# An attention layer and two expert layers on one core: float64 weights loaded from ScalarE's queue, a second cast of the keys, values one item later, sums in pinned steps

## The chip, the cores and the metric

One core of a Trainium2 chip runs the whole program in one launch. The metric is device time in microseconds (us), the median of several runs; lower is better. Engines are named as in the profile: PE (TensorE matmuls), PEld (its weight loads), DVE (VectorE), ACT (ScalarE), POOL (GpSimd), SP (SyncE, which here only issues DMAs).

## The reference

Three layers follow each other. The first is causal attention with a decay: per head a bias built from a running sum of max(s, 0), clipped at zero, is added to the scaled scores.

```python
scores = scale * np.matmul(q, k.transpose(0, 1, 3, 2))      # q, k, v: (2, 8, 576, 64)
cum = np.cumsum(np.maximum(s, 0.0), axis=-1)
bias = -(cum[:, :, :, None] - cum[:, :, None, :])
scores = np.where(causal, -1000000000.0, scores + np.minimum(bias, 0.0))
attn = softmax(scores); x = np.matmul(attn, v)              # then to (1152, 512)
h = x @ w_in; x = np.maximum(0.01 * h, h) @ w_out           # w_in 512x2048, float64 on input
p = domain_probs / (domain_probs.sum(-1, keepdims=True) + 1e-09)
out = sum(p[:, e:e+1] * (np.maximum(x @ w1[e], 0.0) @ w2[e]) for e in range(4))
```

The weights w_in and w_out arrive as float64 and are read as pairs of 32-bit words; the rest is float32.

## The kernel before

**Precision.** Products run in a reduced-precision float32 format. An operand that needs full precision is kept as two terms, hi (a cast by ACT) and lo (the operand less hi, by POOL or DVE), and a product is three matmuls. In the attention's second half the scores put the terms into one tile: `ks` holds the keys' hi in partitions 0 to 63 and their lo in 64 to 127, `kd` holds the hi again in 0 to 63 and the two decay rows behind it, `qs` the queries.

**Attention.** A unit is a batch and a pair of heads (`of_unit`). Units 0 to 7 do the first 256 queries, units 8 to 15 the other 320. A unit's work is cut into items, one tile of queries by one head: four in each of the first eight units, six in the others. `attention()` walks over the items; in turn i it runs the scores of item i, the exponentials of item i - 1, the transposes of item i - 3, the values of item i - 4 and the finish of item i - 6 (`STEPS`), and yields three times, where the caller puts other work. When a unit starts, the loads of keys and values two units on are issued on SP; two turns later `split_keys` makes the next unit's terms at once: three casts or differences, then a DMA on SP that copies the keys' hi from `ks` to `kd`, then the decay rows.

**Weights of the first expert layer.** Sixteen pieces of 128x1024 float64 (`stream`) are loaded to `r64` (two buffers) in two DMAs each by `fetch64`, on SP. `converted` rebuilds float32 from the two words in five steps (ACT, then three times DVE, then the split into hi and lo and a store to the DRAM scratch `w_f32`, on SP). `supply` runs through them; the main block at the end of the function steps it between the items. For the second token group the float32 pieces are read back from `w_f32` and combined to seven sums (`seven`), on POOL.

**The order.** While `fixed` is set every instruction keeps the order in which the code issues it on its engine; the order is thus written by hand for the attention and the first token group's pass through the first expert layer. After that `fixed` is cleared, and a scheduler orders all but what `keep_in_program_order` names. `idling(2)` issues two matmuls on zeros into the unused tile `nothing`; before the change it does so in the turns up to 7.

**Paired tokens.** The second expert layer, and the second token group in the first, use products of half-size blocks of which seven do the work of eight. `paired_steps(s, ...)` makes the seven token operands `t7` from an activation: four sums on DVE and three casts with differences, twice. It runs for the attention's output (s = 1, in the main block, in steps), for the first token group's result (`paired_tokens(0, y_t[0], t7early)`, called at step 12 of `mlps(phases[1])`) and for the second's (`paired_tokens(1, y_t[1], t7pool)`). `paired_up` forms the products; its evictions on DVE are named `tmp` and `ps_u`.

Of the kernel before, what the change touches and what calls it, by code (L numbers as in the profile page):

```python
# [19 lines left out]
def attention_moe_moe2(ctx: ExitStack, tc: tile.TileContext, q, k, v, s, w_in, w_out, probs, w1, w2, out):  # L20
# [89 lines left out]
    def fetch64(n):  # L110

        src, (rows, _) = stream[n][:2]
        r64 = r64p.tile([P, 1024, 2], U32, tag="r64", name="r64")
        r64s.append(r64)
        for i in range(2):
            a, c = slice(i * rows // 2, (i + 1) * rows // 2), slice(i * 512, (i + 1) * 512)
            nc.sync.dma_start(r64[:, c].rearrange("p (a b) t -> p a (b t)", a=rows // 2), src[:, a])
            yield

    def converted(n):  # L120
# [17 lines left out]
        nc.sync.dma_start(w_f32[unit], raw)  # L138
        yield

    def supply():

        for n in range(2 * DFF // P // 2):
            yield from converted(n)
            if len(r64s) < 2 * DFF // P // 2:
                for _ in fetch64(len(r64s)):
                    pass
# [151 lines left out]
    def paired_steps(s, of, pool):  # L299
# [3 lines left out]
        for k in range(2):  # L303
# [6 lines left out]
            nc.vector.tensor_tensor(sums[:, 3], b22, b12, ALU.subtract)  # L310
            nc.vector.tensor_tensor(sums[:, 0], b21, sums[:, 2], ALU.subtract)
# [236 lines left out]
    def split_keys(n):  # L548

        qr, kr = k_raw.pop(n)  # L550
        qs = q_s[n % 2]
        nc.scalar.copy(qs[:, 0], qr)
        nc.gpsimd.tensor_tensor(qs[:D, 1], qr[:D], f32(qs[:D, 0]), ALU.subtract)
        ks = ap.tile([P, 2, S], F32R, tag="ks", name="ks")
        nc.scalar.copy(ks[:D], kr)
        nc.gpsimd.tensor_tensor(ks[D:], kr, f32(ks[:D]), ALU.subtract)
        kd = ap.tile([P, 2, S], F32R, tag="kd", name="kd")
        nc.sync.dma_start(f32(kd[:D]), f32(ks[:D]))
        k_split[n] = ks, kd, qs
        decay(n, kd)  # L560
# [11 lines left out]
    class Unit:  # L572
# [36 lines left out]
        def transposes(self, i, j):  # L609
            z = self.z.pop((i, j))  # L610
            pv = self.pv[i, j] = ap.tile([P, QT, P], F32, tag="pv", name="pv", bufs=3)[:, : i + 1]
# [45 lines left out]
    STEPS = ((Unit.scores, 0), (Unit.exps, 1), (Unit.transposes, 3), (Unit.values, 4), (Unit.finish, 6))  # L657

    def attention():

        items, starts, n = [], {}, 0
        i = 0
        while n < units or i < len(items) + 6:
            if n < units and i == len(items):
# [3 lines left out]
                if n + 2 < units and n + 2 != 2 * NP:  # L668
                    load_keys(n + 2)
                    load_values(n + 2)  # L670
# [4 lines left out]
                if n + 2 == 2 * NP:  # L675
                    load_values(n + 2)
                n += 1
            if 2 * NP <= n < units and i == starts[n - 1] + 2:
                split_keys(n)
            for step, lag in STEPS:  # L680
# [3 lines left out]
                if lag in (1, 3, 6):  # L684
# [11 lines left out]
    with ExitStack() as phase:  # L696
# [5 lines left out]
        with tc.tile_pool(name="early", bufs=1) as early:  # L702
            ones = pads(early)
            cumulative()
            loads = (x for n in range(2) for x in fetch64(n))
            main = mlps(phases[0])

            for at_ in range(3 * 64):
# [5 lines left out]
                if at_ % 3 == 1:  # L714
                    if i < 8:
# [92 lines left out]
```

## Time and profile before

| | |
|---|---|
| median of 3 runs | 759.5 us (759.05 to 760.18) |
| the profiled execution | 758.02 us, its span 756.2 us |
| mean granted TensorE clock | 0.981 of full speed |
| busy PE / PEld | 718.1 us (95%) / 649.6 us (86%) |
| busy DVE / ACT / POOL | 415.5 (55%) / 321.0 (42%) / 322.8 us (43%) |
| moved by DMA | 66.50 MB, mean 88 GB/s |
| chain that ended last | PE 80%, DVE 6%, ACT 6%, issue 3%, DMA 3%, POOL 1% |

The page's strip of 40 slices (18.9 us each) shows PE under 9 tenths in slices 2, 4, 14, 15, 17 and the last, and at 9 in all others; the granted clock is under 9 tenths in slices 2, 4 and 14. Shares over the whole span therefore say little: the attention fills the first 227 us, the hand-over to the second token group runs to some 312 us, and the rest is matmul behind matmul. Windows and timelines of these stages are what is read. All lines of the kernel's engine calls carry the number of the recording helper (L43), so tiles tell the places apart.

### The profile page before, as it was taken

To read this page: it belongs to the slowest core of one execution; us is meant where nothing else is said; L and a number is where in the kernel's file an instruction comes from. 1 tells how busy PE (TensorE), PEld (TensorE's weight loads), DVE (VectorE), ACT (ScalarE), POOL (GpSimd) and SP (SyncE) were. 2 spreads that over 40 slices of the span, in tenths; PEclk is the share of its full clock that TensorE was granted. 3 is DMA by queue.
4 is the path that set the end of the run, shared out by engine and by line. 5 is a ranking of instruction groups with operands and counts; after the bars stand their busy time and mean duration, and the time that the engine had idled before them with its cause. 6 is when DMAs were issued, how large, how long until landed. Compare 5 with 4: busy or idle time off the path is not lost.

```text
span 756.2 us, 11325 instructions
## 1 busy us (share of the span) xinstructions
PE 718.1 (95%) x4340; PEld 649.6 (86%) x4340; DVE 415.5 (55%) x850; ACT 321.0 (42%) x635; POOL 322.8 (43%) x250
## 2 busy tenths in 40 slices
PE   9694999999999889899999999999999999999997
PEld 8573789888887679899998998988989889898996
DVE  4654765757658766644574454544535445354452
ACT  4563877676564465543343231412314123142210
POOL 4122544434218758867427261462614526144200
PEclk9897999999999899999999999999999999999999
DMA  5795567664333222221212120111101111020002
GB/s 146 203 216 136 164 150 191 190 177 156 123 128 129 68 85 84 84 84 57 57 48 65 45 67 1 56 56 54 59 1 57 56 55 56 1 60 25 1 29 97
DMA packets 40346, 66.50 MB, mean 88 GB/s; under 512 B 4228, under 2 KB 23204, under 8 KB 40292
## 3 DMA queue, kind: packets, MB, share of 16 engines
q1 hardware_dynamic: 40292, 65.78, 30.0%
q8 instruction: 34, 0.56, 0.3%
q14 instruction: 20, 0.16, 0.1%
HBM read 52.58 MB, written 10.82 MB: 84 GB/s over the span
## 4 chain that ended last, share of the span: by engine, by line
PE 80%; DVE 6%; ACT 6%; issue 3%; DMA 3%; POOL 1%; SPq 0%; ACTq 0%; POOLq 0%; DVEq 0%
PE ps_d L43 35%; PE ps_u L43 32%; PE ps_o L43 5%; PE ps_sc L43 3%; PE ps_pt L43 3%; DVE raw L43 2%; PE nothing L43 1%; DMA kd<-ks 1%; DVE sums L43 1%; DVE t L43 1%; ACT w L43 1%; DMA r<-in_moe_w_in_dram 1%; ACT ht L43 1%; ACT raw L43 1%; ACT t L43 1%
## 5 line engine op out<-in xcount | busy, mean ns | idle before, releaser
L43 POOL TENSOR_TENSOR w<-raw,w 128x1024 fp32r<-128x1024 f32 (+2 forms) x88 | 147.5, 1690 | 350.8 <-ACT w L43 328.5
L43 PE MATMUL ps_u<-t,w 128*128 128x320 f32 (+1 forms) x1680 | 239.1, 300 | 5.5 <-DVE tmp L43 2.6
L43 PEld LDWEIGHTS ps_u<-t,w 128*128 128x128 f32 x1680 | 234.7, 190 | 9.9 <-DVE tmp L43 3.1
L43 PE MATMUL ps_d<-w,ht 128*128 128x512 f32 x864 | 203.3, 391 | 0.0
L43 PEld LDWEIGHTS ps_d<-w,ht 128*128 128x128 f32 x864 | 160.2, 188 | 31.9
L43 ACT ACTIVATE ht<-ps_u 128x320 fp32r<-128x320 f32 (+2 forms) x176 | 74.2, 433 | 164.3 <-DVE ps_u L43 133.5
L43 PE MATMUL ps_d<-ht,w 128*128 128x320 f32 (+1 forms) x576 | 114.1, 347 | 4.3 <-DVE ht L43 2.1
L43 ACT CAST w<-raw 128x1024 fp32r<-128x1024 f32 (+2 forms) x88 | 64.0, 757 | 97.8 <-PE ps_d L43 77.0
L43 DVE SCALAR_TENSOR_TENSOR oacc<-ps_d,pn,oacc 128x512 f32<-128x512 f32 x63 | 47.3, 751 | 104.3 <-PE ps_d L43 104.3
L43 PEld LDWEIGHTS ps_d<-ht,w 128*128 128x128 f32 x576 | 93.0, 192 | 12.5 <-DVE ht L43 2.9
L43 PEld LDWEIGHTS ps_o<-vs,pv 128*128 128x128 f32 x480 | 64.9, 195 | 12.4 <-ACT pv L43 3.7
L43 DVE TENSOR_TENSOR ps_u<-ps_u,tmp 128x320 f32<-128x320 f32 (+1 forms) x120 | 56.1, 471 | 26.7 <-PE ps_u L43 25.2
L43 PE MATMUL ps_o<-vs,pv 128*128 128x65 f32 x480 | 64.4, 271 | 4.9 <-ACT pv L43 2.2
L43 DVE SCALAR_TENSOR_TENSOR ht<-ps_u,ht 128x320 fp32r<-128x320 f32 (+1 forms) x128 | 56.4, 453 | 22.8 <-ACT ht L43 21.3
L43 DVE CUSTOM_DVE_ANT_0 z<-ps_sc,mask 128x256 f32<-128x256 f32 (+4 forms) x80 | 40.7, 513 | 39.9 <-PE ps_sc L43 31.5
L43 POOL TENSOR_TENSOR w<-sums,w 128x1024 fp32r<-128x1024 f32 x24 | 57.8, 2408 | 6.8 <-ACT w L43 6.8
L43 DVE TENSOR_TENSOR tmp<-ps_u,tmp 128x320 f32<-128x320 f32 (+1 forms) x80 | 36.7, 464 | 41.0 <-PE ps_u L43 39.1
L43 ACT ACTIVATE z<-z,mn 128x256 f32<-128x256 f32 (+4 forms) x80 | 48.5, 607 | 22.8 <-DVE mn L43 22.7
L43 PE MATMUL ps_u<-x,w 128*128 128x512 f32 x192 | 57.8, 416 | 0.1
L43 ACT COPY pv<-ps_pt 128x512 f32<-128x512 f32 (+3 forms) x96 | 38.8, 422 | 24.1 <-PE ps_pt L43 23.8
L43 PE MATMUL ps_pt<-ident,z 128*128 128x128 f32 x240 | 41.2, 279 | 6.5 <-ACT pv L43 6.3
L43 DVE TENSOR_TENSOR ht<-ps_u,ht 128x320 fp32r<-128x320 f32 (+1 forms) x48 | 26.5, 555 | 35.6 <-ACT ps_u L43 35.6
(71 smaller groups left out, 628.7 us busy)
## 6 DMA issues: line engine op xcount, KB each, us to landing
raw<-in_moe_w_dram SPq DMA_DIRECT2D x32, 512.0 KB
r<-in_moe_w_in_dram SPq DMA_DIRECT2D x16, 512.0 KB
w_f<-raw SPq DMA_DIRECT2D x16, 512.0 KB
r<-in_moe_w_out_dram SPq DMA_DIRECT2D x16, 512.0 KB
raw<-w_f SPq DMA_DIRECT2D x16, 512.0 KB
qr<-in_q_dram SPq DMA_DIRECT2D x16, 160.0 KB
kr<-in_k_dram SPq DMA_DIRECT2D x8, 288.0 KB
kd<-ks SPq DMA_DIRECT2D x8, 288.0 KB
```

Source lines behind the costliest of these rows:

```text
L43: ins = call(*args, **kw)
```

## The change

- `fetch64` issues one DMA of 1 MB in place of two of 512 KB, and issues it on ACT; the stores to `w_f32` move to ACT as well. The first two loads come in turns 1 and 5 of the attention.
- `split_keys` becomes a generator of three steps, run in three turns that follow each other. The decay rows come first, and the copy by DMA is replaced by a second cast of `kr` on ACT. The first one (unit 8) runs during unit 6 in place of unit 7.
- The values of an item run five turns behind its scores in place of four, the finish seven in place of six; `pv` has four buffers in place of three. The loads of values are issued two turns into a unit.
- In the first phase the idle matmuls run up to turn 19, the conversion starts at turn 9 in place of 8, and the expert layer may start at turn 21 in place of 20.
- All subtractions of `paired_steps` are pinned to program order, and for the first token group's result the steps are spread, one every sixth step from step 12.

```diff
     def fetch64(n):
         src, (rows, _) = stream[n][:2]
         r64 = r64p.tile([P, 1024, 2], U32, tag="r64", name="r64")
         r64s.append(r64)
-        for i in range(2):
-            a, c = slice(i * rows // 2, (i + 1) * rows // 2), slice(i * 512, (i + 1) * 512)
-            nc.sync.dma_start(r64[:, c].rearrange("p (a b) t -> p a (b t)", a=rows // 2), src[:, a])
-            yield
+        nc.scalar.dma_start(r64.rearrange("p (a b) t -> p a (b t)", a=rows), src)
...
         ready.append(split_w(raw, shape, False))
-        nc.sync.dma_start(w_f32[unit], raw)
+        nc.scalar.dma_start(w_f32[unit], raw)
...
-            tc.keep_in_program_order(nc.vector.tensor_tensor(sums[:, 1], b12, b11, ALU.subtract))
-            nc.vector.tensor_tensor(sums[:, 2], b22, sums[:, 1], ALU.subtract)
+            def subtract(*args):
+                tc.keep_in_program_order(nc.vector.tensor_tensor(*args, ALU.subtract))
+
+            subtract(sums[:, 1], b12, b11)
+            subtract(sums[:, 2], b22, sums[:, 1])
...
                 nc.scalar.copy(hi, x)
-                nc.vector.tensor_tensor(lo, x, f32(hi), ALU.subtract)
+                subtract(lo, x, f32(hi))
...
         qs = q_s[n % 2]
+        ks, kd = (ap.tile([P, 2, S], F32R, tag=tag, name=tag) for tag in ("ks", "kd"))
+        decay(n, kd)
         nc.scalar.copy(qs[:, 0], qr)
         nc.gpsimd.tensor_tensor(qs[:D, 1], qr[:D], f32(qs[:D, 0]), ALU.subtract)
-        ks = ap.tile([P, 2, S], F32R, tag="ks", name="ks")
+        yield
         nc.scalar.copy(ks[:D], kr)
         nc.gpsimd.tensor_tensor(ks[D:], kr, f32(ks[:D]), ALU.subtract)
-        kd = ap.tile([P, 2, S], F32R, tag="kd", name="kd")
-        nc.sync.dma_start(f32(kd[:D]), f32(ks[:D]))
+        yield
+        nc.scalar.copy(kd[:D], kr)
         k_split[n] = ks, kd, qs
-        decay(n, kd)
+        yield
...
-    STEPS = ((Unit.scores, 0), (Unit.exps, 1), (Unit.transposes, 3), (Unit.values, 4), (Unit.finish, 6))
+    STEPS = ((Unit.scores, 0), (Unit.exps, 1), (Unit.transposes, 3), (Unit.values, 5), (Unit.finish, 7))
...
-            if 2 * NP <= n < units and i == starts[n - 1] + 2:
-                split_keys(n)
+            if n < units - 1 and i == starts[n - 1] + 2:
+                load_values(n + 1)
+            if i == starts[n - 1] + 2 and 2 * NP - 1 <= n < units and n != 2 * NP:
+                split = split_keys(max(n, 2 * NP))
+            next(split, None)
...
-                    if i < 8:
+                    if i < 20:
                         idling(2)
-                    elif i >= 20 and opened < 3 * (done // 2) and (opened < 6 or i >= 30):
+                    elif i >= 21 and opened < 3 * (done // 2) and (opened < 6 or i >= 30):
...
+        tokens = paired_steps(0, y_t[0], t7early)
         for i, _ in enumerate(mlps(phases[1])):
-            if i == 12:
-                paired_tokens(0, y_t[0], t7early)
+            if i >= 12 and i % 6 == 0:
+                next(tokens, None)
```

The order in which the instructions now stand shows three places. The first is ACT at the split of unit 8's keys (`r` is the float64 tile, `kr` and `qr` the loaded keys and queries). Before:

```order
L43 ACTIVATE raw<-r_515 128x1024
L43 CAST qs<-qr 128x640
L43 CAST ks<-kr 64x1152
L43 ACTIVATE z<-z,mn 128x256
L43 COPY pv<-ps_pt 128x128
L43 ACTIVATE z<-z,mn 128x128
L43 COPY pv<-ps_pt 128x256
L43 ACTIVATE z<-z,mn 128x128
L43 COPY pv<-ps_pt 128x256
L43 ACTIVATE z<-z,mn 128x576
```

and with the change:

```order
L43 CAST qs<-qr 128x640
L43 ACTIVATE z<-z,mn 128x256
L43 COPY pv<-ps_pt 128x128
L43 CAST x_102<-ps_x 128x256
L43 CAST ks<-kr 64x1152
L43 ACTIVATE z<-z,mn 128x128
L43 COPY pv<-ps_pt 128x256
L43 CAST w<-raw 128x1024
L43 DMA w_f_73<-raw 128x1024
L43 CAST kd<-kr 64x1152
L43 ACTIVATE z<-z,mn 128x128
L43 COPY pv<-ps_pt 128x256
```

Before, the two casts stand three exponentials ahead of unit 8's first (128x576), and the copy to `kd` is a DMA on SP. Now there are three casts, each in a turn of its own, with five further exponentials of units 6 and 7 between the last and unit 8's first; the store of the converted weights stands among them on ACT.

The second is ACT after the attention, where the last two `ht` of the first token group's pass are evicted (`ps_u`), while `t` and `w_25..` are the operands of the second token group. Before:

```order
L43 CAST w_2577<-raw 128x256
L43 CAST w<-raw 128x1024
L43 CAST w_2565<-sums 128x1024
L43 ACTIVATE ht<-ps_u 128x512
L43 ACTIVATE ps_u<-ps_u 128x512
L43 CAST t_1_2457<-sums 128x4x320
L43 ACTIVATE ht<-ps_u 128x512
L43 ACTIVATE ps_u<-ps_u 128x512
L43 CAST w_2577<-sums 128x1024
L43 CAST t_1_2457<-x_98 128x2x320
```

and with the change:

```order
L43 CAST w_2573<-sums 128x1024
L43 CAST w<-raw 128x1024
L43 DMA w_f_73<-raw 128x1024
L43 CAST t_1_2467<-x_98 128x320
L43 ACTIVATE ht<-ps_u 128x512
L43 ACTIVATE ps_u<-ps_u 128x512
L43 CAST t_1_2467<-sums 128x4x320
L43 CAST w_2585<-sums 128x1024
L43 CAST t_1_2467<-x_98 128x2x320
L43 CAST t_1_2467<-x_98 128x320
L43 ACTIVATE ht<-ps_u 128x512
L43 ACTIVATE ps_u<-ps_u 128x512
```

The second eviction stood two casts ahead of the second cast of `sums`; it now stands behind that cast and two more, and the store has joined the row.

The third is DVE in the same hand-over, ahead of the second token group's first and third block of products, whose evictions begin with `tmp` (`t_0` is made of the first token group's result, `y`; `t_1` of the attention's output). At the first block, before:

```order
L43 TENSOR_TENSOR y_1237<-ps_d,y_1237 128x512
L43 TENSOR_TENSOR t_1_2457<-sums,t_1_2457 128x4x320
L43 TENSOR_TENSOR t_0_2961<-y_1237,t_0_2961 128x2x256
L43 TENSOR_TENSOR t_0_2961<-y_1237,t_0_2961 128x256
L43 TENSOR_TENSOR t_0_2961<-y_1237,t_0_2961 128x2x256
L43 TENSOR_TENSOR t_0_2961<-y_1237,t_0_2961 128x256
L43 TENSOR_TENSOR tmp<-ps_u_2692,tmp 128x320
L43 TENSOR_TENSOR tmp<-ps_u_2763,tmp 128x320
```

and with the change:

```order
L43 TENSOR_TENSOR t_1_2467<-x_98,t_1_2467 128x320
L43 TENSOR_TENSOR y_1275<-ps_d,y_1275 128x512
L43 TENSOR_TENSOR t_1_2467<-sums,t_1_2467 128x4x320
L43 TENSOR_TENSOR tmp<-ps_u_2700,tmp 128x320
L43 TENSOR_TENSOR tmp<-ps_u_2771,tmp 128x320
L43 TENSOR_TENSOR tmp<-ps_u_2701,tmp 128x320
L43 TENSOR_TENSOR tmp<-ps_u_2772,tmp 128x320
```

The four differences `t_0<-y` are gone from this place. They now stand further back, where before only the sums stood; ahead of the third block, before:

```order
L43 TENSOR_TENSOR sums<-y_1237 128x256 x2
L43 TENSOR_TENSOR sums<-y_1237,sums 128x256 x2
L43 TENSOR_TENSOR t_0_2961<-sums,t_0_2961 128x4x256
L43 TENSOR_TENSOR sums<-y_1237 128x256
L43 TENSOR_TENSOR sums<-y_1237,sums 128x256 x2
L43 TENSOR_TENSOR tmp<-ps_u_3069,tmp 128x320
L43 TENSOR_TENSOR tmp<-ps_u_3070,tmp 128x320
```

and with the change:

```order
L43 TENSOR_TENSOR sums<-y_1275 128x256
L43 TENSOR_TENSOR sums<-y_1275,sums 128x256
L43 TENSOR_TENSOR sums<-y_1275 128x256
L43 TENSOR_TENSOR sums<-y_1275,sums 128x256
L43 TENSOR_TENSOR t_0_2969<-y_1275,t_0_2969 128x2x256
L43 TENSOR_TENSOR t_0_2969<-y_1275,t_0_2969 128x256
L43 TENSOR_TENSOR tmp<-ps_u_3064,tmp 128x320
L43 TENSOR_TENSOR tmp<-ps_u_3065,tmp 128x320
```

Seven sums and one wide difference stood there; four sums and two narrower differences do now, and the others follow among the evictions of the next block.

## Rows read from the trace of the kernel before

**Rows 1.** Windows by stage: us, busy us (x instructions) of each engine, PEclk, DMA share, GB/s.

```profile
14.00:58.00 44.00, 35.93 (x220) 29.53 (x219) 25.80 (x90) 27.76 (x68) 7.99 (x4) 0.92 0.85 218
58.00:69.00 11.00, 2.13 (x9) 1.67 (x9) 3.79 (x6) 1.51 (x6) 3.26 (x2) 0.67 0.86 200
...
80.00:227.00 147.00, 142.03 (x930) 125.73 (x930) 94.95 (x203) 104.17 (x178) 53.19 (x23) 1.00 0.55 160
...
312.00:756.00 444.00, 440.15 (x2643) 404.75 (x2641) 214.91 (x435) 131.13 (x276) 180.62 (x149) 1.00 0.16 49
```

**Rows 2.** Timeline of PE at the first split unit: start us, us, tile [idle before <-releaser].

```profile
61.39 0.47 PE L43 MATMUL ps_sc<-ks,qs 128*128 128x448 f32 x1 [2.26 <-POOL ks L43]
67.78 0.74 PE L43 MATMUL ps_sc<-kd,qs 66*128 66x448 f32 x1 [5.92 <-DMA kd<-ks]
```

**Rows 3.** Windows again, short stretches in which the granted clock (PEclk) is under 1.

```profile
24.00:32.00 8.00, 6.41 (x29) 5.14 (x28) 5.68 (x18) 4.16 (x9) 2.36 (x1) 0.57 0.55 162
...
66.00:70.00 4.00, 2.22 (x8) 1.99 (x9) 0.99 (x4) 0.62 (x2) 0.00 (x0) 0.50 0.28 57
70.00:74.00 4.00, 4.00 (x23) 3.55 (x22) 1.46 (x6) 1.65 (x4) 0.00 (x0) 0.75 0.02 4
...
308.00:312.00 4.00, 4.00 (x20) 4.00 (x19) 2.59 (x6) 4.00 (x10) 2.72 (x2) 0.63 0.00 0
```

**Rows 4.** Groups by line and form: xcount, busy us, mean ns of one.

```profile
L43 PE MATMUL nothing<-idle 128*128 128x128 f32 x76 | 12.9, 330 | 1.1 <-DVE idle L43 1.1
...
L43 ACT CAST ks<-kr 64x1152 fp32r<-64x1152 f32 x8 | 9.3, 1156 | 0.0
```

**Rows 5.** Tiles r and w_f, their DMA issues: ns min/median/max of one issue.

```profile
L43 SPq DMA_DIRECT2D r<-in_moe_w_in_dram x16: 367/465/1430, 11.8 to 194.3; - x16
...
L43 SPq DMA_DIRECT2D w_f<-raw x16: 320/338/535, 28.4 to 240.8; - x16
```

**Rows 6.** Timelines of ACT and PE around 21 to 23 us.

```profile
21.23 1.12 ACT L43 ACTIVATE raw<-r 128x1024 f32<-128x1024 f32 x1 [2.46 <-DMA r<-in_moe_w_in_dram]
...
22.95 0.33 PE L43 MATMUL ps_pt<-ident,z 128*128 128x128 f32 x1 [2.27 <-ACT pv L43]
```

**Rows 7.** Waits of PE from 80 to 227 us: us in total, times, longest.

```profile
PE ps_pt L43 <- ACT pv L43: 2.8, 4, 1.1
```

**Rows 8.** Timelines of ACT, DVE and PE from 243 to 262 us.

```profile
243.63 1.06 ACT L43 CAST w<-sums 128x1024 fp32r<-128x1024 f32 x1 [1.70 <-POOL sums L43]
...
246.73 0.60 ACT L43 ACTIVATE ht<-ps_u 128x512 fp32r<-128x512 f32 x1
...
253.18 1.04 ACT L43 CAST w<-sums 128x1024 fp32r<-128x1024 f32 x1 [5.36 <-POOL sums L43]
254.13 1.08 ACT L43 CAST t<-x 128x640 fp32r<-128x640 f32 x2
...
249.53 0.68 DVE L43 TENSOR_TENSOR ht<-ps_u,ht 128x512 fp32r<-128x512 f32 x1
...
250.27 11.53 PE L43 MATMUL ps_d<-ht,w 128*128 128x512 f32 x37 [2.15 <-DVE ht L43]
```

**Rows 9.** DVE's timeline at 264 us, and PE's waits from 262 to 280 us.

```profile
264.43 5.81 DVE L43 TENSOR_TENSOR t<-y,t 128x512 fp32r<-128x512 f32 x4 [0.50 <-ACT t L43]
...
PE ps_u L43 <- ACT w L43: 2.2, 2, 1.4
PE ps_u L43 <- DVE tmp L43: 0.9, 1, 0.9
```

**Rows 10.** DVE's timeline at 299 us, and PE's waits from 280 to 312 us.

```profile
299.61 5.07 DVE L43 TENSOR_TENSOR sums<-y,sums 128x256 f32<-128x256 f32 x2
...
PE ps_u L43 <- DVE tmp L43: 1.7, 1, 1.7
PE ps_u L43 <- DVE ps_u L43: 0.6, 1, 0.6
```

**Rows 11.** Timeline of PE at the start of the last layer.

```profile
375.59 19.03 PE L43 MATMUL ps_u<-t,w 128*128 128x256 f32 x144
```

More of the change, by code (lines that the diff above doesn't have):

```diff
@@ L145, in supply @@
             if len(r64s) < 2 * DFF // P // 2:
-                for _ in fetch64(len(r64s)):
-                    pass
+                fetch64(len(r64s))
     def load_w(src, shape, unit):
@@ L306, in paired_steps @@
             sums = scratch.tile([P, 4 * 320], F32, tag="scratch", name="sums")[:, : 4 * n].rearrange("p (s t) -> p s t", s=4)
-            tc.keep_in_program_order(nc.vector.tensor_tensor(sums[:, 1], b12, b11, ALU.subtract))
-            nc.vector.tensor_tensor(sums[:, 2], b22, sums[:, 1], ALU.subtract)
+            def subtract(*args):
+                tc.keep_in_program_order(nc.vector.tensor_tensor(*args, ALU.subtract))
+            subtract(sums[:, 1], b12, b11)
+            subtract(sums[:, 2], b22, sums[:, 1])
             yield
-            nc.vector.tensor_tensor(sums[:, 3], b22, b12, ALU.subtract)
-            nc.vector.tensor_tensor(sums[:, 0], b21, sums[:, 2], ALU.subtract)
+            subtract(sums[:, 3], b22, b12)
+            subtract(sums[:, 0], b21, sums[:, 2])
             yield
@@ L654, in attention_moe_moe2 @@
     done = 0
-    STEPS = ((Unit.scores, 0), (Unit.exps, 1), (Unit.transposes, 3), (Unit.values, 4), (Unit.finish, 6))
+    STEPS = ((Unit.scores, 0), (Unit.exps, 1), (Unit.transposes, 3), (Unit.values, 5), (Unit.finish, 7))
     def attention():
         items, starts, n = [], {}, 0
-        i = 0
-        while n < units or i < len(items) + 6:
+        i, split = 0, iter(())
+        while n < units or i < len(items) + 7:
             if n < units and i == len(items):
@@ L683, in attention @@
                     step(u, *of)
-                if lag in (1, 3, 6):
+                if lag in (1, 3, 7):
                     yield i
@@ L704, in attention_moe_moe2 @@
             cumulative()
-            loads = (x for n in range(2) for x in fetch64(n))
             main = mlps(phases[0])
@@ L720, in attention_moe_moe2 @@
                 if at_ % 3 == 2:
-                    if i % 3 == 1:
-                        next(loads, None)
-                    if i >= 8 and (i < 18 or i % 2):
+                    if i in (1, 5):
+                        fetch64(i // 4)
+                    if i >= 9 and (i < 19 or i % 2):
                         next(units_of_w)
@@ L759, in attention_moe_moe2 @@
         hidden_pool(phase, 3)
+        tokens = paired_steps(0, y_t[0], t7early)
         for i, _ in enumerate(mlps(phases[1])):
-            if i == 12:
-                paired_tokens(0, y_t[0], t7early)
+            if i >= 12 and i % 6 == 0:
+                next(tokens, None)
+        for _ in tokens:
+            pass
     paired_tokens(1, y_t[1], t7pool)
```

5 lines of the change are left out of this document (1 added, 4 removed).

## The prediction

> **What bounds the kernel now.** I read the windows by stage first. From 312 us to the end PE is busy 440.15 of 444 us at full clock [rows 1]: that stretch is matmul behind matmul, and this change takes none away. From 80 to 227 us, the attention's second half, PE is busy 142.03 of 147 us, so at most 5 us are to be had there. The two stretches before are different: PE is busy 35.93 of 44 us from 14 to 58 us, and 2.13 of 11 from 58 to 69 us [rows 1]. The timeline of PE shows the second hole: the first matmul of unit 8 waited 2.26 us for the keys' second term, and the second one 5.92 us for the DMA that copies the first term from `ks` to `kd` [rows 2]. The short windows show what such a hole leaves behind: the granted clock is 0.50, the lower of its two levels, from 66 to 70 us, and 0.75 on average in the next 4 us [rows 3]. Around 22 us PE waited 2.27 us for a copy that ACT made late, since ACT itself stood 2.46 us waiting for the first float64 piece [rows 6]; from 24 to 32 us the clock is 0.57 [rows 3]. After the attention three smaller holes follow, at 250, 262 to 280 and 280 to 312 us [rows 8 to 10], where PE waits for evictions that stand behind other work on ACT or DVE.
>
> **The change part by part.** All sums are against the profiled execution, 758.02 us.
>
> *First split.* The copy by DMA is gone, and the order puts unit 8's three casts a unit earlier, with five exponentials between. Both waits go, 2.26 + 5.92 = 8.2 us [rows 2], and with them the slow stretch: 2.22 us of work at 0.50 and 4.00 at 0.75 lose 1.1 + 1.0 us [rows 3]. Taken: -10.3. Bounds: -10.3, and -5.9 where the second term stays late and the clock with it. What could be late next is the decay rows' DMA; it has no producer but the scratch written at the start, and is now issued first.
>
> *From 14 to 58 us.* The first load starts in turn 1 from ACT, not behind the key loads on SP. If it is in time, the 2.27 us go, and of the 6.41 us of work at 0.57 some 2.8 us are won back: -5.0. Against that ACT gets new work here: five loads, three stores and one cast of keys. A load issue took 0.465 us for half a piece and a store 0.338 [rows 5]; the whole piece in one issue I put between 0.465 and 0.93. With 1.156 us for the cast [rows 4] that is 4.5 to 6.8 us, and ACT is idle 16.2 of the 44 us [rows 1], which hides most; I charge 1.5. The 24 further idle matmuls cost 12.9 / 76 = 0.17 us each, 4.1 us [rows 4], inside 8.1 us of PE's idle time: nothing, unless that idle time goes. The values one turn later loosen PE's waits for ACT; I count nothing for it here. Taken: -3.5. Bounds: -8.1, when PE has no idle time left, and +4.1, when the piece is as late as now and the idle matmuls are paid.
>
> *From 80 to 227 us.* Values five turns behind, with a fourth buffer, can take away PE's waits for ACT's copies, 2.8 us [rows 7]. ACT gets eleven loads, eleven stores and six casts: 15.8 to 20.9 us by the same prices. It is busy 104.17 of 147 us [rows 1] and would be at 125 at most, still under PE. But it is in order: a cast or an issue in front of an eviction delays that eviction. I charge 1.8. Taken: -1.0. Bounds: -2.8 and +4.2, a fifth of ACT's new work on PE's path. Loads of values that come two turns later are still a unit ahead: nothing. The loads that leave SP take waits for conversions with them; no PE wait in rows 7 is for these, so I count nothing.
>
> *The last `ht` of the first token group.* Here the new order speaks against the change. The second cast of `sums` on ACT began at 253.18 us, 9.55 us after the first, as POOL made the sums in between [rows 8]. The second `ht` stood ahead of it, at 246.73 us; now it stands behind it and two further casts: 253.18 + 1.04 + 1.08 = 255.3 us, and with 0.60 on ACT and 0.68 on DVE PE gets its operand at 256.6 in place of 250.27 us: +6.3. ACT's first cast waited 1.70 us for POOL; the read-back of the weights, which POOL needs, no longer stands behind a store on SP, so that much can go: taken +4.5. Bounds: +6.3, and 0 where POOL runs so much faster that ACT doesn't wait.
>
> *Pinned sums.* Four differences of 5.81 us stood ahead of the first `tmp` on DVE, and PE then waited 0.9 us for `tmp` and 2.2 us for casts that ACT had behind those evictions [rows 9]. They are moved back: -3.1. Ahead of the third block the sums stood, two of them alone 5.07 us, and PE waited 1.7 + 0.6 us [rows 10] and then ran 4.00 us at 0.63 [rows 3], 1.5 us lost. Now less stands there: -3.8. The rest follows among evictions of a stretch in which DVE is busy 214.91 of 444 us [rows 1]. Bounds for both together: -6.9, and 0 where the moved work makes PE wait elsewhere.
>
> *The last layer's first operands* are pinned too, so their sums start only after the eighth eviction, where before some stood between. PE's 144 matmuls there run 19.03 us without a wait [rows 11]; three DVE steps of about 0.68 us [rows 8] are what could come late. Taken +0.5, bounds 0 and +2.0.
>
> Sum: -10.3 - 3.5 - 1.0 + 4.5 - 3.1 - 3.8 + 0.5 = -16.7, so 741.3 us. The median of the runs stands 1.5 us above the profiled execution; **predicted: 743 us**.
>
> **The rivals.** *A: the loads compete.* From 14 to 58 us the DMA engines are at 0.85 of their time, 218 GB/s [rows 1]. A piece of 1 MB in a second queue then takes its bandwidth from the keys and values that the turns need, the next piece is late as the first was, and that stretch gains nothing: I set +2 there (half of its upper bound) and 0 from 80 to 227 us. -10.3 + 2 + 4.5 - 3.1 - 3.8 + 0.5 = -10.2: 749 us. For it: the 0.85. Against it: the copies of the keys leave, and three stretches in the windows have DMA time free. The Trainium skill, DMA: Bandwidth & Descriptors, Issuing engines are not separate DMA queues, says the same: DMAs of all issuing engines run on the same 16 DMA engines and interleave, and issuing from several saves only the time to issue. By that rule the time would be this rival's; no row here shows two queues at once, so it has a chance of its own.
>
> *B: all covers hold.* PE's idle time from 14 to 58 us goes (-8.1), the copies' waits go (-2.8), and the late `ht` is covered (0): -10.3 - 8.1 - 2.8 - 3.1 - 3.8 + 0.5 = -27.6, 732 us. For it: ACT and DVE are busy under 28 of 44 us. Against it: the row of casts ahead of `ht` is there in the order.
>
> *C: ACT becomes the bound, slower.* Sixteen loads, sixteen stores and eight casts are 22.1 to 29.5 us on the engine that makes the exponentials, the copies and the evictions. Without gains in the two attention stretches the other terms give -12.2; from 12.2 us of ACT's new work on PE's path the kernel is slower, and with three quarters of the larger sum, 22 us, it would be +10: 769 us. For it: in-order issue, and a DMA issue that waits for its counter holds ACT. Against it: ACT at 104.17 of 147 us, and PE's waits for it there are 2.8 us now.
>
> *D: the split isn't what held unit 8.* From 58 to 69 us the DMA engines are at 0.86 [rows 1]; if what crowds them also delays the decay rows, the hole stays by some 8 us: 751 us.
>
> **How the numbers follow.** Chances: the forecast 0.50, A 0.22, B 0.13, C 0.07, D 0.06, and 0.02 for the terms cancelling. The forecast's own range is 737 to 750 us. The whole range, 733 to 754 us, takes in A and D with 4 us above, and B's near half; C and B's far half, 0.07 + 0.07, are left out, and some room is kept for terms that I can't see. A difference within 0.2% (1.5 us) is about what a measurement of this kernel can't tell from none. Faster by more: forecast, A, B and D, 0.91; same 0.02; slower C, 0.07.
>
> **What would show it.** Right: unit 8's first matmuls without a wait on a DMA or on POOL, full clock in the windows after it, unit 8 starting 12 us or more earlier; no PE wait for `tmp` after the hand-over; a longer wait than 2.15 us for the last `ht`. Wrong: a DMA as what ends ACT's waits ahead of `raw`, in more than one place (A); ACT's busy time over 130 of PE's stretch of 147 us with PE idle over 10 us (C); a wait for the decay rows at unit 8 (D). If PE's time from 312 us to the end grows by over 3 us, the pinned sums cost what I set at nothing.

## The result, and the profile after

The changed kernel takes 749.7 us (median, 749.36 to 750.41) where the kernel before takes 759.27 beside it: a ratio of 0.9876, with a 95% interval of 0.9859 to 0.9893. That is 9.6 us faster. The prediction was 743 us, 16.5 us faster, with a range of 733 to 754: the side is right and the time lies in the range, but only 6 parts in 10 of the gain came. The profiled execution has a span of 747.8 us (before: 756.2), 8.4 us less.

The windows by stage come first, as in [rows 1] and [rows 3]; the columns are those.

```profile
14.00:58.00 44.00, 38.90 (x271) 34.68 (x270) 28.41 (x94) 30.07 (x71) 11.29 (x5) 0.95 0.90 244
...
50.00:54.00 4.00, 1.92 (x15) 1.54 (x14) 0.34 (x4) 4.00 (x10) 3.86 (x2) 0.96 0.98 329
54.00:58.00 4.00, 3.94 (x14) 3.56 (x15) 2.56 (x7) 1.25 (x5) 0.00 (x0) 0.50 0.93 254
58.00:62.00 4.00, 4.00 (x18) 3.49 (x18) 2.52 (x10) 2.28 (x5) 0.17 (x1) 0.69 0.31 90
80.00:227.00 147.00, 134.72 (x870) 117.19 (x869) 103.03 (x190) 103.68 (x172) 53.55 (x25) 1.00 0.46 143
262.00:280.00 18.00, 16.95 (x114) 16.46 (x113) 8.11 (x19) 11.59 (x29) 12.22 (x10) 1.00 0.26 89
280.00:312.00 32.00, 32.00 (x220) 32.00 (x219) 19.90 (x37) 19.65 (x44) 28.45 (x24) 1.00 0.30 99
```

From 14 to 58 us PE is busy 38.90 us in place of 35.93. From 262 to 312 us it is busy 48.95 of 50 us, where the kernel before has 44.52 in the same windows, with the waits of [rows 9, 10]: the hand-over is nearly closed. Two stretches are worse. From 80 to 227 us PE is busy 134.72 us, 7.3 less than in [rows 1] (4.3 of it is one wait at the end; the changed kernel is some 5 us ahead there, so the window doesn't hold quite the same work), and from 50 to 54 us there is a new hole, with the clock at 0.50 and 0.69 in the eight microseconds behind it.

The timeline of PE shows where both are (start, duration, tile, and in brackets the wait before it):

```profile
51.92 0.33 PE L43 MATMUL ps_pt<-ident,z 128*128 128x128 f32 x1 [1.22 <-ACT pv L43]
54.06 0.69 PE L43 MATMUL ps_pt<-ident,z 128*128 128x128 f32 x2 [0.92 <-ACT pv L43]
56.11 0.72 PE L43 MATMUL ps_sc<-ks,qs 128*128 128x448 f32 x1
56.63 0.57 PE L43 MATMUL ps_sc<-kd,qs 66*128 66x448 f32 x1
...
227.08 10.06 PE L43 MATMUL ps_d<-ht,w 128*128 128x512 f32 x36 [4.34 <-DVE y L43]
236.97 5.60 PE L43 MATMUL ps_u<-x,w 128*128 128x512 f32 x24
247.63 0.73 PE L43 MATMUL ps_d<-ht,w 128*128 128x512 f32 x2 [3.02 <-ACT ht L43]
248.84 10.01 PE L43 MATMUL ps_d<-ht,w 128*128 128x512 f32 x37 [0.48 <-DVE ht L43]
```

Unit 8's first matmuls, at 56.11 and 56.63 us, wait for nothing: both waits of [rows 2] are gone. But PE waits 1.22 and 0.92 us for ACT's copies just ahead, and 4.34 us at the attention's end for DVE's `y`, a wait that the prediction didn't have at all. Behind it 36 matmuls take 10.06 us, since part of them runs at the lower clock (0.59 on average from 227 to 231 us).

Laid against each other by the same matmuls, the two profiled executions give this table. Unit 8's start is taken without its own 2.26 us of wait before, 59.13 us.

| stretch of PE's program | before | after | difference | the prediction's terms |
|---|---|---|---|---|
| from 14 us to unit 8's first scores | 45.13 | 42.11 | -3.0 | -3.5 |
| unit 8 to the last matmul ahead of the 36 | 169.36 | 166.62 | -2.7 | -10.3 and -1.0 |
| from there to the 24 matmuls `ps_u<-x,w` | 9.30 | 14.24 | +4.9 | none |
| to the last `ht`'s matmuls | 12.48 | 11.87 | -0.6 | +4.5 |
| to the first paired product | 11.36 | 9.85 | -1.5 | none |
| to the first `ps_d<-ht,w` of the paired tokens | 16.84 | 14.49 | -2.4 | -3.1 |
| to the `ps_d` behind the third block | 34.63 | 30.21 | -4.4 | -3.8 |
| to the end | 443.10 | 444.41 | +1.3 | +0.5 |
| sum | 756.2 - 14 | 747.8 - 14 | -8.4 | -16.7 |

Three terms came about as forecast, the early load and the two of the pinned sums. The second and third lines carry the miss, 13.5 us together; the fourth came out 5.1 us better than its term.

### The profile page after: what moved, and what is told of

It is laid out like the page before. It is cut to its first block, busy times and chain, and to the rows that moved or that the text cites. A ratio compares the mean times of both kernels' runs of the same rounds, so it can differ in the third digit from the quotient of the medians.

```text
span 747.8 us, 11394 instructions
## 1 busy us (share of the span) xinstructions
PE 718.2 (96%) x4388; PEld 651.2 (87%) x4388; DVE 418.8 (56%) x850; ACT 330.0 (44%) x643; POOL 323.2 (43%) x250
## 4 chain that ended last, share of the span: by engine, by line
PE 83%; DVE 5%; ACT 5%; POOL 3%; issue 3%; ACTq 0%; POOLq 0%; DVEq 0%
PE ps_d L43 38%; PE ps_u L43 32%; PE ps_o L43 5%; PE ps_sc L43 4%; PE ps_pt L43 3%; DVE raw L43 2%; PE nothing L43 2%; POOL w L43 2%; POOL sums L43 1%; ACT w L43 1%; ACT z L43 1%; DVE z L43 1%; ACT raw L43 1%; ACT pv L43 1%; DVE t L43 1%
## 5 line engine op out<-in xcount | busy, mean ns | idle before, releaser
L43 DVE SCALAR_TENSOR_TENSOR raw<-r,raw 128x1024 uint32<-128x1024 uint32 x32 | 45.7, 1429 | 0.2
```

Of the source, the lines that this page charges most:

```text
L43: ins = call(*args, **kw)
```

## The experiments

Two theories for the attention stood against each other at first: P, that one step of the conversion stands at the wrong place, and Q, that ACT's new DMA issues delay its work.

**e1, the conversion one turn later.** The changed kernel had begun the conversion at turn 9 where it was 8. Since the attention's first half also ends one turn later, and the conversion runs in every odd turn by then, it enters the second half one step ahead of where it was. One line undoes this:

```diff
-                    if i >= 9 and (i < 19 or i % 2):
+                    if i >= 10 and (i < 19 or i % 2):
```

> The changed kernel with the conversion started at turn 10 in place of 9, so that it enters the attention's second half one step less far on, as in the kernel before. Theory P (the phase of the conversion): the 4.3 us wait of PE for y at the attention's end, and the slower clock in the 36 matmuls behind it (10.06 us for 8.46), come from the cast of the converted weights, which now stands ahead of the last ht on ACT; the wait falls to about 1 us, the 36 matmuls take 8.5 us, and the time falls by 4 to 5 us, to 745 us. Theory Q (ACT's queue: the loads, stores and the third cast that ACT now issues delay its evictions wherever they stand): the wait at the end stays over 3 us, 749 to 750 us.

Measured: 744.54 us (740.08 to 746.99), ratio 0.9815 (0.977 to 0.986). The stretch from the attention's last transposes to the 24 matmuls takes 10.50 us in place of 15.42. So P holds at the attention's end. Its mechanism is to be seen in the changed kernel's timelines of ACT and DVE there:

```profile
221.16 1.05 ACT L43 CAST w<-raw 128x1024 fp32r<-128x1024 f32 x1 [5.42 <-DVE raw L43]
222.11 0.59 ACT L43 ACTIVATE ht<-ps_u 128x512 fp32r<-128x512 f32 x1
...
223.11 1.13 ACT L43 ACTIVATE raw<-r 128x1024 f32<-128x1024 f32 x1
...
234.02 1.06 ACT L43 CAST w<-sums 128x1024 fp32r<-128x1024 f32 x1 [4.95 <-POOL sums L43]
...
235.81 1.06 ACT L43 CAST w<-raw 128x1024 fp32r<-128x1024 f32 x1 [0.73 <-PE ps_d L43]
...
245.06 1.04 ACT L43 CAST w<-sums 128x1024 fp32r<-128x1024 f32 x1 [2.83 <-POOL sums L43]
...
246.99 0.59 ACT L43 ACTIVATE ht<-ps_u 128x512 fp32r<-128x512 f32 x1
```

```profile
223.22 0.69 DVE L43 TENSOR_TENSOR ht<-ps_u,ht 128x512 fp32r<-128x512 f32 x1 [2.15 <-ACT ps_u L43]
224.27 2.06 DVE L43 TENSOR_SCALAR raw<-raw 128x1024 f32<-128x1024 f32 x2 [0.36 <-ACT raw L43]
226.25 0.68 DVE L43 TENSOR_TENSOR y<-ps_d,y 128x512 f32<-128x512 f32 x1
```

The cast of the converted weights waits 5.42 us for DVE's last step on `raw`, and the eviction `ht` stands behind it, so does the next `raw`, and on DVE two steps on that `raw` (2.06 us) stand ahead of `y`. PE waits for that `y`. In the kernel before, the evictions stood ahead of the cast:

```profile
225.42 0.60 ACT L43 ACTIVATE ht<-ps_u 128x512 fp32r<-128x512 f32 x1 [2.84 <-PE ps_u L43]
...
228.07 1.04 ACT L43 CAST w<-raw 128x1024 fp32r<-128x1024 f32 x1 [1.56 <-DVE raw L43]
```

The last four of the changed kernel's ACT rows belong to the last `ht` and are read further down.

The same line also nearly closes the hole at 50 to 54 us. In e1 PE is busy 3.51 us there, where the changed kernel has 1.92; its longest wait for a copy by ACT is 0.49 us, and unit 8 begins at 52.78 us, 3.3 us earlier.

**e5, the step back in the second half only**, to part the two things that e1 had moved at once:

```diff
-        owed = given = 0
+        owed, given = 0, -1.0
```

> The changed kernel with the conversion one step back from the attention's second half on only (the first half keeps the change's turns). In e1 two things moved at once: unit 8 began 3.3 us earlier and the stretch from the last transposes of the attention to the 24 matmuls behind it took 10.5 us in place of 15.4. Theory P says they are independent: here unit 8 begins at 56 us as in the changed kernel and the last stretch takes 10.5 us: some 745 us. Rival: the end depends on when the attention got there, and stays at 15.4 us: 749 to 750 us.

Measured: 742.2 us (741.70 to 745.07), ratio 0.9801 (0.9755 to 0.9846). Unit 8 begins at 56.08 us, as in the changed kernel, and the last stretch takes 10.49 us:

```profile
218.50 0.94 PE L43 MATMUL ps_d<-ht,w 128*128 128x512 f32 x3
220.44 8.47 PE L43 MATMUL ps_d<-ht,w 128*128 128x512 f32 x36 [1.00 <-ACT x L43]
228.74 5.60 PE L43 MATMUL ps_u<-x,w 128*128 128x512 f32 x24
```

P is shown for the attention's end. The hole at 50 to 54 us stays (PE is busy 1.88 us). More came than was expected: PE's idle time from unit 8 to the attention's end fell too, by 2.5 us, as these two windows (unit 8's first scores to the attention's last matmul) show, first of the changed kernel, then of e5. The third is of the kernel with the split alone (e3, below).

```profile
56.11:222.73 166.62, 156.85 (x1007) 136.64 (x1006) 112.81 (x224) 119.18 (x200) 59.04 (x26) 0.99 0.46 142
```

```profile
56.08:219.44 163.36, 156.12 (x1007) 136.61 (x1006) 105.24 (x225) 118.94 (x200) 59.49 (x25) 0.99 0.46 143
```

```profile
60.85:223.71 162.86, 154.59 (x1003) 136.02 (x1001) 109.63 (x226) 118.04 (x201) 57.26 (x25) 0.99 0.50 146
```

Busy against length: 9.77 us idle in the changed kernel, 7.24 in e5, 8.27 in e3. In the kernel before it is 12.16 in the same stretch, 6.24 without the 5.92 us for the copy. This idle time repeats well: the changed kernel's second profile (e9) has 9.77 us too, and e4, which is the changed kernel up to here, 9.76. In e1 it is 9.27, so the same step back brings only 0.5 us where the first half moves with it. Of PE's waits from unit 8 on, those for DVE's `mn` are 2.7 us in the changed kernel and 1.3 in e5, and one of 1.1 for a copy by ACT ahead of `ps_x` is gone.

**e2, the loads and stores on SP again**:

```diff
-        nc.scalar.dma_start(r64.rearrange("p (a b) t -> p a (b t)", a=rows), src)
+        nc.sync.dma_start(r64.rearrange("p (a b) t -> p a (b t)", a=rows), src)
-        nc.scalar.dma_start(w_f32[unit], raw)
+        nc.sync.dma_start(w_f32[unit], raw)
```

> The changed kernel with the sixteen float64 loads and the sixteen stores issued on SP again, everything else as it is. Theory Q: ACT is rid of some 12 us of issues; the idle time of PE from unit 8 to the attention's end falls from 9.8 us to the 6.3 us of the kernel before (without its wait for the copy), and the pile of ACT work at 47 to 55 us shrinks: 744 to 747 us. Theory P: the issues beside ACT's work cost nothing that PE sees, the wait for y stays at 4.3 us, and the time is within 1.5 us of 749.7; where SP's order makes the float64 loads late, up to 4 us more.

Measured: 754.3 us (750.15 to 756.07), ratio 0.9937 (0.9904 to 0.9969). Its two executions with the changed kernel's mean clock, 0.990, take 750.15 and 750.73 us; the others are at 0.979 to 0.984. The profiled one has a span of 749.0, 1.2 more than the changed kernel's, and an idle time of 9.61 us from unit 8 on where that has 9.77. So 32 issues on ACT cost PE nothing there, and theory Q falls. The medians are 4.6 to 5.2 us above the changed kernel's all the same: three of e2's five executions have a lower clock, and none of the changed kernel's ten has. Whether the queue bears on the clock is open. The stall at 21 us stays away as well (PE is busy 9.93 us from 14 to 24 us, 7.31 in the kernel before), so ACT's queue didn't cure it. Two things are left that no run parts: the first piece is issued whole in turn 1, not in halves in turns 1 and 4, and the conversion begins a turn later.

**e3, the kernel before with the new split alone** (the generator of three steps with its second cast, its call and the early first one, as in the change's diff).

> The kernel before with the new split of the keys alone (three steps, a second cast in place of the copy, unit 8's a unit earlier). By the prediction's first term 10.3 us less, 749 us, with unit 8's two waits gone and the clock full behind it. Rival: in the changed kernel two waits of PE for ACT's copies (1.22 and 0.92 us) and the clock at 0.50 and 0.69 for 8 us stand just ahead of and behind unit 8; if the new casts on ACT make them, they are here too, and the gain is 8.2 + 2.1 - 2.1 - 3.2 = 5 us, 754 us.

Measured: 752.31 us (749.68 to 757.69), ratio 0.9952 (0.9923 to 0.9981), 4.7 us faster. The ten executions spread from 749.7 to 757.7 us, and the interval of the ratio leaves 1.4 to 5.8 us. The rival's size is right, for another reason than it gave. The clock is full around unit 8, but PE's idle time in the rest of the second half is 2.0 us more (8.27 against 6.24), and the clock is at the lower level from 34 to 41 us in this execution, for some 3 us. The waits of unit 8 are gone, 8.2 us; less than that arrives.

**e7, the copy by DMA back, in e1's place**:

```diff
-        nc.scalar.copy(kd[:D], kr)
+        nc.sync.dma_start(f32(kd[:D]), f32(ks[:D]))
```

> e1 with the DMA copy of the keys' first term back in the third step in place of the second cast. Theory R (eight more casts of 1.15 us on ACT are what raised PE's idle time in the second half from 6.3 to 8.3 us in the kernel with the split alone): idle 7 to 7.5 us here, unit 8 without a wait for the copy since it is issued a unit earlier, span 736 to 737 us. Rival: the copy is late again, PE waits up to 5.9 us for it at unit 8 with a slower clock behind it: 742 to 746 us.

Measured: 742.36 us (738.52 to 743.71), ratio 0.9787 (0.9736 to 0.9838). Unit 8 waits 0.15 us for the copy, which is issued at 47.76 us and used at 53.31, and PE's idle time from unit 8 on is 6.94 us where e1 has 9.27: theory R holds. The span of the profiled execution is 741.9 us all the same, since its clock is low behind 62 us; that is taken up at the end.

**e10 and e12, the old split with all other parts as changed**, once as it is and once with the loads and stores on SP (e2's edit on top).

```diff
-            if i == starts[n - 1] + 2 and 2 * NP - 1 <= n < units and n != 2 * NP:
-                split = split_keys(max(n, 2 * NP))
-            next(split, None)
+            if 2 * NP <= n < units and i == starts[n - 1] + 2:
+                split_keys(n)
```

(with `split_keys` as before the change).

> The changed kernel with the old split of the keys (all at once, a unit before its use, copy by DMA), all other parts as changed. By the sums without the clock the split alone saves 7.6 us, and all other parts lose 3.3 us in the attention and 3.3 at its end and gain 5.6 in the hand-over and lose 1.3 behind it: 7 to 8 us over the changed kernel without the clock, and with unit 8's hole back some 757 to 760 us, no faster than the kernel before. Rival: the prediction's terms, in which the other parts are worth 6.4 us: 750 to 754 us.

> e10 (old split, copy by DMA, all else as changed) with the float64 loads and the stores issued on SP again. In e10 PE waited only 0.93 us for the copy at unit 8, which took 5.0 us from its issue, where it took 9.6 and PE waited 5.92 before the change. Theory V (the queue): the copy was late because it stood on SP's queue behind a float64 load; with the load there again it takes over 8 us, PE waits 4 us or more at unit 8, and the time is 754 to 758 us. Theory W (the time of the load): the queue is indifferent, the load now merely starts 3 to 4 us ahead of the copy where it was 2.4, and there are fewer other transfers beside it: the copy takes 5 to 6 us, PE waits under 2 us, 750 to 753 us.

Measured: e10 751.47 us (746.38 to 752.74), ratio 0.9906 (0.9871 to 0.9941); e12 754.25 us (749.54 to 756.06), ratio 0.9957 (0.9935 to 0.998). The other parts are worth 6.3 us by themselves (757.75 to 751.47), the rival's number. The sum by which e10 was to be 757 us or more took it that unit 8's hole comes back with the old split, and it doesn't: unit 8's two waits are nearly gone. But the changed kernel's hole just ahead is here as well, as a single wait of 2.02 us. PE, then the issues on SP (SPq), of e10:

```profile
53.24 0.69 PE L43 MATMUL ps_pt<-ident,z 128*128 128x128 f32 x2 [2.02 <-ACT pv L43]
...
55.97 0.74 PE L43 MATMUL ps_sc<-ks,qs 128*128 128x448 f32 x1 [0.44 <-POOL ks L43]
57.64 0.74 PE L43 MATMUL ps_sc<-kd,qs 66*128 66x448 f32 x1 [0.93 <-DMA kd<-ks]
```

```profile
52.65 0.53 SPq L43 DMA_DIRECT2D kd<-ks  x1
```

And of e12:

```profile
56.19 0.74 PE L43 MATMUL ps_sc<-ks,qs 128*128 128x448 f32 x1 [1.15 <-POOL ks L43]
60.00 0.74 PE L43 MATMUL ps_sc<-kd,qs 66*128 66x448 f32 x1 [3.08 <-DMA kd<-ks]
```

```profile
48.63 0.54 SPq L43 DMA_DIRECT2D r<-in_moe_w_out_dram  x1
...
52.88 0.54 SPq L43 DMA_DIRECT2D kd<-ks  x1
```

From its issue to the matmul that waits for it the copy takes 5.0 us in e10, 7.1 in e12, and 9.7 in the kernel before (58.11 to 67.78). In e12 a float64 load of 1 MB stands in front of it on SP's queue, issued 4.3 us earlier; in e10 that load is in ACT's queue, issued at 49.03 us. Giving loads and stores back to SP's queue thus costs the copy 2.1 us. The other 2.6 us, from e12 to the kernel before, where the load was issued in two halves 2.4 us ahead, aren't parted further. Neither V (4 us of wait or more) nor W (under 2) has it alone: PE waits 3.08 us in e12.

From unit 8's first scores to the attention's last matmul PE idles 6.95 us in e10, 6.02 without its wait for the copy, and 6.20 in e12 reckoned so. The window of e10:

```profile
55.97:219.77 163.80, 156.85 (x1005) 137.38 (x1005) 110.64 (x225) 111.67 (x193) 60.20 (x26) 0.98 0.52 158
```

That is the kernel before's idle time (6.24), with the conversion's place of the changed kernel: the whole of the changed kernel's further idle time there comes with the new split.

The Trainium skill, DMA: Bandwidth & Descriptors, Issuing engines are not separate DMA queues, says that DMAs of all issuing engines share the same 16 DMA engines and interleave, so that several issuers save only the time to issue. By it e2 is as fast as the changed kernel, which its idle time bears out (9.61 and 9.77 us) and its median does not. By that sentence taken alone, which says nothing of the order inside one queue, e12's copy would land when e10's does, and here the measurement differs, by 2.1 us in one profile of each: behind a load of 1 MB in the same queue a copy of 288 KB is later than beside it in another.

**e4, the paired sums as before** (`subtract` without pins but on the first sum, and `paired_tokens(0, y_t[0], t7early)` at step 12).

> The changed kernel with paired_steps and its call at step 12 as before the change (no pins but the first, no spreading). If the pinned, spread sums are what shortened the hand-over by 2.4 and 4.4 us and lengthened the rest by 1.3: 5.5 us more, 755 us, and the waits for tmp at both blocks are back. Rival: the hand-over is shorter because POOL and ACT got to it earlier, with the read-back of the weights no longer behind stores: within 1.5 us of 749.7.

Measured: 755.78 us (754.75 to 758.55), ratio 0.9981 (0.9965 to 0.9997), 6.1 to 6.7 us over the changed kernel's medians. The two stretches that the sums had shortened, the sixth and seventh of the table, take 17.03 and 35.93 us in place of 14.49 and 30.21, and PE's waits are those of [rows 9, 10] again (waits of PE from 262 to 330 us):

```profile
PE ps_u L43 <- DVE tmp L43: 2.6, 2, 1.7
PE ps_u L43 <- ACT w L43: 2.2, 2, 1.4
PE ps_u L43 <- DVE ps_u L43: 0.6, 1, 0.6
```

**e6, the values four turns behind** (`STEPS`, loop bound, the third yield and `pv`'s buffers as before).

> The changed kernel with the values four turns behind, the finish six and three buffers of pv, as before the change; the attention is one turn shorter by that, so that the conversion enters the second half as in e1. Against e1 (span 738.3 us, PE idle 9.3 us from unit 8 to the attention's end): if the later values keep PE from waiting for ACT's copies, the idle time here is 2 to 3 us more and the time 741 to 743 us in the profile; if they don't matter, the idle time is within 1 us and the span 737 to 740 us.

Measured: 745.57 us (742.26 to 749.87), ratio 0.9841 (0.978 to 0.9901), span 740.5 us, idle time 8.25 us from unit 8 on. That is 1.0 less than e1's 9.27 and not 2 to 3 more, so no gain of the later values shows there; unit 8 begins at 56.82 us, close to the changed kernel's 56.11 and not to e1's 52.78. This doesn't settle what the later values are worth in the whole.

**e8, the idle matmuls up to turn 7 only** (`if i < 8:` in e1).

> e1 with the idle matmuls up to turn 7 only, 48 fewer. If they are what keeps the granted clock at 1.00 from 24 to 40 us: a stretch at 0.5 to 0.7 there, unit 8 2 to 3 us later, span 740 to 742 us. If they only fill gaps and cost nothing: within 1 us of e1. If they cost time (6.8 us of PE's work): unit 8 up to 2 us earlier, 736 us.

Measured: 744.18 us (740.74 to 749.2), ratio 0.9829 (0.9758 to 0.99). The clock is 0.79 from 24 to 32 us, 1.00 in e1, and unit 8 begins at 53.03 us where e1's does at 52.78. The other profiles agree: from 24 to 32 us the clock is 1.00 in all eleven with the idle matmuls up to turn 19, and 0.57, 0.57 and 0.79 in the three with them up to turn 7 (the kernel before, e3 and e8). So the matmuls hold the clock, and the time is as e1's within the runs' spread.

**e9 and e11, the changed kernel again and the best version**, on one chip. e11 has e5's edit and e7's.

> The changed kernel as it is, on the chip and beside the runs of the next two: 749 to 751 us. Between runs the time should go with the stretches at the lower clock, as in the earlier runs; if it doesn't, the sums that leave the clock out are not to be trusted.

> The changed kernel with the conversion one step back in the second half (as in e5) and the DMA copy in place of the second cast (as in e7). Theory P and theory R together: without the cast the pile of ACT's work at 47 to 55 us is 1.2 us smaller, PE's 2.1 us hole there shrinks below 1.5, the last stretch of the attention takes 10.5 us, and PE's idle time from unit 8 on is under 7 us: 737 to 741 us, over 1% below the changed kernel. Rival: the slow clock falls in another stretch instead, 742 to 745 us, no better than e5.

Measured: e9 749.12 us (748.68 to 750.52), ratio 0.9893 (0.9863 to 0.9922); e11 737.36 us (736.04 to 740.17), ratio 0.974 (0.9708 to 0.9771): 11.8 us under the changed kernel. That is 5 us below e5 and e7 as well, which ran on another chip; the intervals of the ratios just overlap. Its windows at the hole and from unit 8's first scores to the attention's last matmul:

```profile
50.00:54.00 4.00, 2.89 (x20) 2.24 (x20) 1.36 (x6) 3.92 (x11) 3.54 (x2) 1.00 1.06 311
...
53.90:213.78 159.88, 154.11 (x1008) 134.96 (x1006) 105.78 (x226) 112.24 (x194) 59.82 (x25) 1.00 0.55 165
```

The hole at 50 to 54 us is 1.11 us, under the 1.5 that was expected, the clock is 1.00 from 54 to 62 us, the idle time is 5.77 us, and the last stretch takes 10.49.

## Why the prediction was right, and where it was wrong

That the time lies in the range owes something to luck: two lines of the table are worse than their terms by 13.5 us together, and one is better by 5.1. Of the signs that the prediction named for being right, three came: no wait at unit 8, none for `tmp`, a longer one for the last `ht`. Two didn't: the clock behind unit 8 is not full, and unit 8's two first matmuls start 5.3 and 11.2 us earlier, not 12.

**First split (-10.3): mis-sized, and not the split's alone.** The two waits went, as said, 8.2 us. The step that failed is "Both waits go [...] and with them the slow stretch": it took the new casts for free, and the clock for won. In the changed kernel ACT has this to do ahead of unit 8:

```profile
47.60 1.15 ACT L43 CAST ks<-kr 64x1152 fp32r<-64x1152 f32 x1
...
49.21 1.05 ACT L43 CAST w<-raw 128x1024 fp32r<-128x1024 f32 x1
...
50.16 1.16 ACT L43 CAST kd<-kr 64x1152 fp32r<-64x1152 f32 x1
...
52.32 1.15 ACT L43 ACTIVATE raw<-r 128x1024 f32<-128x1024 f32 x1
```

Two casts of keys, and a cast and a `raw` of the conversion: 4.5 us of work within 5.9 us, the copies `pv` between them late, and PE waits the 2.1 us shown above. Behind that 3.94 + 4.00 us of its work run at 0.50 and 0.69: 2.0 + 1.2 = 3.2 us lost, where the slow stretch of [rows 3] had cost 2.1. This hole isn't the split's: with the old one it is there (e10, 2.02 us of wait), and with the new one and the conversion a turn later it isn't (e1). It comes of the conversion's start, whose steps fall among the casts of keys; the second cast adds to it, as e11, without that cast, waits 1.11 us. What the split costs is idle time behind unit 8's start, 9.77 us in place of 6.02 (e10). By itself (e3) the split is worth 4.7 us. On top of the other parts it is worth 2.4 (e10's 751.47 to e9's 749.12), since those remove most of the same waits: 0.44 + 0.93 us of them are left in e10. The sum counted the waits as if nothing else in the change touched them, and the second cast, which costs PE 2.3 or 1.5 us of idle time from unit 8 on (e7 against e1, e11 against e5), as nothing behind it.

**From 14 to 58 us (-3.5): right in size**, -3.0, and the 2.1 us of the new hole are in that. The wait for the first float64 piece is gone and the clock is 1.00 from 24 to 32 us. ACT's queue didn't do it (e2). The prediction gave the whole gain of clock to the early load; with that load and without the further idle matmuls (e8) the clock is 0.79, so part of it is theirs, which it set at nothing. A count was off: a float32 matmul has two records here (38 idle matmuls in the kernel before have 76), so the 24 further ones are 48 records (76 to 124, 12.9 to 19.7 us), 6.8 us and not 4.1. They lay in idle time, as said, and e8 finds no difference in time.

**From 80 to 227 us (-1.0): wrong in sign.** Of the "15.8 to 20.9 us by the same prices" ACT got, the issues cost nothing (e2), and the casts cost more than the 1.8 charged. Against the kernel before PE idles 3.5 us more from unit 8 on, the wait for the copy left out (9.77 against 6.24). All of it comes with the new split: with the old one and all else as changed PE idles 6.02 us (e10), so the later values and the moved loads leave this time as it was, where -2.8 had been hoped for. Mending the second cast brings 2.3 or 1.5 us of it back, mending the conversion's place 2.5 (e5) or 0.5 (e1). These single gains don't add up; with both mended, in e11, the idle time is 5.77, just under the kernel before. The bound of +4.2 held.

**The conversion's start: not priced, +4.9 and the hole.** The prediction has no term for the conversion at turn 9 in place of 8, nor for the first half that ends a turn later. At the attention's end these cost a wait of 4.34 us in place of 1.00, and 10.06 us for 36 matmuls in place of 8.46, at the lower clock. Ahead of unit 8 they cost the hole: in e1, where the turn alone is put back, unit 8 begins 3.3 us earlier. The order shows the step ahead of the evictions, some ten rows above the place that the prediction quoted of ACT; it was read only where there was a term already.

**The last `ht` (+4.5): mechanism right, size wrong.** `ht` stands behind the second cast of `sums` and two more, and PE waits 3.02 + 0.48 us for it, longer than 2.15. But the forecast kept the times of [rows 8], in which POOL has the second sums ready at 253.1 us. The second cast of `sums` began 8.1 us earlier than that, as the attention ended 5.8 us earlier; PE came to this place late, by the 4.9 us above, and ACT and POOL didn't: the last converted weights are cast at 235.81 us, 1.2 ahead of PE's 24 matmuls, where they came 3.1 behind them (240.88 and 237.79), and that second cast is at 245.06. The lower bound of 0, "where POOL runs so much faster", stood nearest to this. And the feared order has the same cause as the wait before it: in e5, with the step back, `ht` (237.31 us) is ahead of the second cast (244.01) again, and the stretch takes 12.36 us, as before the change.

**Pinned sums (-6.9): right.** -2.4 and -4.4 in the table; e4 undoes them, both stretches grow back, and it is 6.1 to 6.7 us slower. The 1.5 us of the line ahead of them is clock: 37 matmuls take 10.01 us where they took 11.53 [rows 8].

**Last layer (+0.5): right in place, larger.** PE waits 1.14 us for `t` before the last 33 of the matmuls that ran without a wait in [rows 11]:

```profile
365.87 14.23 PE L43 MATMUL ps_u<-t,w 128*128 128x256 f32 x111
381.25 5.34 PE L43 MATMUL ps_u<-t,w 128*128 128x320 f32 x33 [1.14 <-DVE t L43]
```

**The rivals.** A's time, 749 us, is the measured one, but A didn't come: from 14 to 58 us no wait of ACT for a float64 piece is in the trace, though the DMA engines are at 0.90. C didn't either: ACT is busy 103.68 of 147 us. D was half right, in that what crowds the DMA engines made the copy late; it had the decay rows wait, and they don't.

## What to carry to other kernels

Price every edit of the order, above all a start moved by one turn: on engines that work in order it can move a step past an eviction. Here it did so at the last eviction before a phase ended, and it let two piles of casts meet on ACT. Two edits that remove the same wait don't add up; ask of each what is left of the wait when only the other is made. Here a copy by DMA beat a cast on a busy engine where it was issued early enough (5.5 us ahead of its use in e7: 0.15 us of wait), and cost a stall where it was issued just in time behind a large load.

## What was not expected of the hardware

The granted clock answers the same hole differently from one profile to the next. e1 and e7, which differ in the copy of the keys, have the same gap (2.38 us busy from 58 to 62), and e7 then runs at 0.50, the lower level, from 66 to 74 us and e1 at full clock. Windows of e1, then e7:

```profile
58.00:62.00 4.00, 2.38 (x18) 1.72 (x17) 3.96 (x8) 3.26 (x6) 2.63 (x2) 1.00 0.54 158
...
66.00:70.00 4.00, 4.00 (x34) 3.82 (x33) 2.25 (x9) 2.24 (x5) 0.00 (x0) 1.00 0.06 13
```

```profile
58.00:62.00 4.00, 2.38 (x16) 1.67 (x15) 3.96 (x8) 3.05 (x7) 2.63 (x2) 1.00 1.07 261
...
66.00:70.00 4.00, 4.00 (x20) 3.91 (x19) 1.31 (x5) 0.59 (x1) 0.00 (x0) 0.50 0.20 62
```

e4 has the changed kernel's hole at 50 to 54 us (1.86 us busy), full clock from 54 to 62 us where the changed kernel is at 0.50 and 0.69, and 0.50 from 66 to 74:

```profile
50.00:54.00 4.00, 1.86 (x15) 1.48 (x14) 0.30 (x2) 4.00 (x10) 3.81 (x2) 1.00 1.07 336
54.00:58.00 4.00, 3.98 (x25) 3.43 (x25) 3.48 (x13) 2.32 (x6) 0.00 (x0) 1.00 0.89 241
...
66.00:70.00 4.00, 4.00 (x20) 3.91 (x19) 0.63 (x2) 2.05 (x3) 1.96 (x1) 0.50 0.68 215
```

This is also most of the spread between runs: e1's four have mean clocks of 0.995, 0.991, 0.984 and 0.983 and take 740.08, 742.41, 746.66 and 746.99 us, while the changed kernel's six in e9 are all at 0.990 and within 1.9 us. One profile's time can thus be off by some 5 us through the clock; PE's idle time is what was compared here for that reason. Why the clock falls late in one run, at once in another and not at all in a third isn't settled by these runs.
